# Routed attention with an MLP behind it: five small moves in an order written by hand

## The chip, the cores and the metric

The kernel runs on one core of a Trainium2 chip. The metric is the device time of one execution in microseconds (us), the median of the runs. The engines are TensorE (PE in the profile, its weight loads PEld), VectorE (DVE), ScalarE (ACT), GpSimd (POOL) and SyncE (SP); the last two mostly issue DMA transfers here.

## The reference

Attention in which every query and key is assigned to one of 16 centroids, and a query sees only the keys of its own cluster; then a layer norm and an MLP with a residual. Everything is float32.

```python
q_assign = argmax(einsum('bhsd,hcd->bhsc', q_n, c_n))     # k likewise
mask = q_assign[:, :, :, None] == k_assign[:, :, None, :]
scores = where(mask, scale * q @ k.T, -1e9)
attn = exp(scores - max); attn = attn / (sum(attn) + 1e-9)
x = (attn @ v) as (B, S, H*D)
xn = (x - mean) / sqrt(var + 1e-6) * g_ln
out = x + max(xn @ w_ch1, 0) @ w_ch2
```

B = 4 batches, H = 8 heads, S = 768 positions, D = 64 (so H*D = 512), hidden width 2048. The two MLP weights arrive as 64-bit floats.

## The kernel before, in words

**Attention.** The work is cut into 16 pairs of heads, n = 0 to 15; pair n belongs to batch n // 4. A pair has two halves ("slots" 0 and 1) of six steps. A step of a half makes one score tile of 128 keys by 384 queries for both heads: `scores` puts two mask products and two q k products into one of three PSUM buffers (`s_ps`), and ScalarE takes the exponential into `e`. `weigh` then multiplies the six tiles with v (`a_ps`), adds them up on VectorE (`es`, L433 and L436) and copies the result (`x`, L445). A half takes TensorE about ten us.

**Preparing the next pair.** While pair n is computed, pair n + 1 is prepared. Its q and k have to be turned so that D lies on the partitions. `prep_transpose` does this in one of two ways. Pairs named in `blocks` are loaded in 32 by 32 blocks, so that one VectorE transpose is enough (L281). The others are turned by six TensorE products with the identity into a score buffer (L286), which ScalarE copies (L291). k takes the first way in all pairs but pair 0. q takes it in pair 1 and in pairs 7 to 15; q of pairs 2 to 6 goes through TensorE, one pair earlier, in slot 1. `prep_sims` (`sim_ps`, L313) needs both; `prep_turn`, `prep_route`, `prep_onehot` (`oh_ps`, L355) and `prep_mask` make the one-hot and mask rows from it (`shade`, L373: on VectorE in pair 0, on ScalarE in the others).

**Closing a pair.** `finish` has four parts: 0 sums `es` over the keys on TensorE (`den_ps`) and sends the sums through DRAM into another layout; 1 takes the reciprocal and brings it back as rows (`rb`); 2 multiplies (`L488`) and stores x^T to DRAM (`xT_d`); 3 transposes and stores x (`x_d`). Parts 2 and 3 of pair n run two pairs later.

**Weights.** 32 chunks are converted from 64-bit to 32-bit floats by six VectorE operations each (`split_weight`, `join_weight`, L246 to L266) and an accumulating DMA. Two chunks go to each of pairs 0 to 6, one to each of pairs 7 to 15 (23 in all), the last nine into the first MLP layer of batch 0 (`within`).

**Norm of batch 0.** It is placed in the attention of later pairs by `put(n, slot, job)`: x^T is loaded as `xn` at pair 6, the statistics (`norm_rows`) follow at pairs 7 to 9, `norm_stats` (mean, square root on ScalarE, reciprocal) at the end of pair 9, `norm_stat_rows` between scores and weighing of pair 10, `norm_apply` at pairs 11 to 14, and the first sums of the MLP at pair 15.

**MLP.** Each layer is written with seven block products instead of eight. In `first_layer` a hidden tile j has seven parts (L761) that accumulate in banks `x_ps`, `y_ps`, `z_ps`; they need sums of x blocks (`x_sum`, L578: t1, t2, t4) and of weight blocks (`w1_sums`, L594: s1 to s4, for tile j made during tile j - 1). `first_units(0, j)` mixes in the conversions. The second layer (L854) follows, with the sums of its weights (`w2t`, L838). The norm of the next batch is hidden behind it.

**Order.** In the attention and in batch 0's first layer the order on TensorE, VectorE and ScalarE is the order of the calls (`manual_schedule`); each engine runs its queue in order. Later only TensorE's order is fixed by hand and a scheduler places the rest. The end of the attention and the start of the MLP read:

```python
finish(len(pairs) - 1, 0)
first_layer(0, 0, 1)
first_layer(0, 0, 2)
first_layer(0, 0, 6)
w1_sums(0, 0, (2, 3))
```

Of the kernel before, what the change touches and what calls it, by code (L numbers as in the profile page):

```python
# [8 lines left out]
F32 = mybir.dt.float32  # L9
# [3 lines left out]
AF = mybir.ActivationFunctionType  # L13
ALU = mybir.AluOpType
# [5 lines left out]
def kernel(  # L20
# [11 lines left out]
    nc = tc.nc  # L32
    B, H, S, D = q.shape
    NCL = centroids.shape[1]
    DM, FF = moe_w_ch1.shape
    P = 128
    NT = S // P
# [5 lines left out]
    NDC = DM // P  # L43
# [7 lines left out]
    xpool = ctx.enter_context(tc.tile_pool(name="xpool", bufs=1))  # L51
    small = ctx.enter_context(tc.tile_pool(name="small", bufs=2))
# [17 lines left out]
    def ps(name, dt=F32, n=512):  # L70
        return pools["t"].tile([P, n], dt, tag="t", name=name)

    pairs = [(b, pr) for b in range(B) for pr in range(NPAIR)]
    loaded = {n: {} for n in range(len(pairs))}

    TWICE = 7

    blocks = {
        (n, name) for n in range(1, len(pairs)) for name in ("qk" if n == 1 or n >= TWICE else "k")
    }  # L80

    def load_blocks(n, name):
# [57 lines left out]
    eps = const.tile([P, 1], F32, name="eps")  # L140
# [231 lines left out]

    def shade(n, out, src, rows):  # L373
        add, factor = far[rows, 0:1], far[rows, 1:2]
        if n:
            nc.scalar.activation(out, src, AF.Identity, bias=add, scale=factor)
        else:
            nc.vector.tensor_scalar(out, src, factor, add, op0=ALU.mult, op1=ALU.add)  # L378
# [10 lines left out]
    late = {}  # L389
# [59 lines left out]
    def finish(n, part):  # L449
        b, pr = pairs[n]  # L450
        if part == 0:
            den = ps_a.tile([P, 512], F32, tag="a", name="den_ps") if n + 1 < len(pairs) else ps("den_ps")
            for j in range(2):
                for g in range(NHALF):
                    r = (j * NHALF + g) * Q
                    nc.tensor.matmul(  # L456
                        den[r : r + Q, :HC], ones, sums[n, g][:, j, :],
                        start=True, stop=True, tile_position=(0, r),
                    )
            if n + 1 < len(pairs):  # L460
                dsb = last.tile([P, HC], F32, tag="dsb", name="dsb", bufs=1)
            else:
                dsb = late["all"][:, 1, :HC]
            nc.scalar.copy(dsb, den[:, :HC])
            flat = dram.tile([P // Q, HC], F32, tag="flat", name="flat")
            nc.gpsimd.dma_start(out=flat, in_=dsb[0:P:Q, :])
            nc.gpsimd.dma_start(
                out=rdens[:, n, :], in_=flat.rearrange("i (p e) -> (i p) e", e=DE)
            )
        elif part == 1:  # L470
            nc.vector.reciprocal(rdens[:, n, :], rdens[:, n, :])
            row = dram.tile([2, S], F32, tag="row", name="row")
            nc.gpsimd.dma_start(
                out=row.rearrange("j (p e) -> (j p) e", e=DE), in_=rdens[:, n, :]
            )
            if n + 1 < len(pairs):
                rb = last.tile([P, S], F32, tag="rb", name="rb", bufs=1)
            else:
                rb = late["all"][:, 2]
            for j in range(2):  # L480
                nc.gpsimd.dma_start(
                    out=rb[j * D : (j + 1) * D, :],
                    in_=row[j : j + 1, :].to_broadcast([D, S]),
                )
            late[n] = rb
        elif part == 2:
            a, x = xs.pop(n), late[n]
            nc.vector.tensor_tensor(x, a, x, ALU.mult)  # L488
            nc.sync.dma_start(out=xT_d[b][pr], in_=x)
        else:  # L490
            x = late.pop(n)

            if n + 1 < len(pairs):
                y = last.tile([P, S], F32, tag="y", name="y")
            else:
                y = late["all"][:, 0]
            nc.vector.transpose(y, x)
            for i in range(P // Q):
                m = pr * P + i * Q
                nc.sync.dma_start(  # L500
                    out=x_d[b].rearrange("t (a r) m -> r (t a) m", r=Q)[:, :, m : m + Q],
                    in_=y[i * Q : (i + 1) * Q].rearrange("r (g f) -> r g f", f=Q),
                )
# [3 lines left out]
    normed = {}  # L507
    rows = {}

    def norm_load(b):  # L510
        xn = xpool.tile([P, NDC, S], F32, tag="xn", name="xn")
        for c in range(NDC):
            nc.sync.dma_start(out=xn[:, c, :], in_=xT_d[b][c])
        mv = small.tile([P, NT, 2], F32, tag="mv", name="mv")
        normed[b] = [xn, mv]

    def rows_load(b, t):
        if t < NT:
# [9 lines left out]
        nc.vector.bn_stats(out=bn, in_=x)  # L528
        nc.vector.bn_aggr(out=mv[:, t, :], in_=bn)

    def norm_stats(b):

        _, mv = normed[b]
        stat = small.tile([P, 2, NT], F32, tag="stat", name="stat")
        nc.scalar.activation(stat[:, 1, :], mv[:, :, 1], AF.Sqrt, bias=eps)
        nc.vector.tensor_copy(stat[:, 0, :], mv[:, :, 0])
        nc.vector.reciprocal(stat[:, 1, :], stat[:, 1, :])
        normed[b][1] = stat

    def norm_stat_rows(b):  # L540
        sp = ps("stat_ps") if b else ps_s.tile([P, 2, 512], F32, tag="s", name="stat_ps")[:, 0]
# [55 lines left out]
    extra = {}  # L597

    def put(n, slot, f, *args):
        extra.setdefault((n, slot), []).append(lambda: f(*args))  # L600

    put(6, 0, norm_load, 0)
    put(6, 1, rows_load, 0, 0)
    put(6, 1, rows_load, 0, 1)
    for t in range(NT):
        put(7 + t // 2, t % 2, norm_rows, 0, t)
    put(9, 1, norm_stats, 0)
    put(10, "between", norm_stat_rows, 0)
    for i in range(2):
        for c in range(NDC):  # L610
            put(11 + 2 * i + c // 2, 1, norm_apply, 0, i, c)
# [10 lines left out]
    slots = per // GROUP  # L622

    convert = {}
    for n in range(len(pairs)):
        for slot in (0, 1) if n < TWICE else (0,):
            convert[n, slot] = len(convert)
    order = {mybir.EngineType.PE, mybir.EngineType.DVE, mybir.EngineType.Activation}
# [36 lines left out]
    with tc.manual_schedule(engines=order | {mybir.EngineType.Pool}):  # L665
        for u in range(len(pairs) * slots):
            n, slot = divmod(u, slots)
            nxt = n + 1 < len(pairs)
            own = range(GROUP * u, GROUP * (u + 1))
            if slot == 0 and not nxt:  # L670
                finish(n - 1, 0)
            if slot == 0 and nxt:
                for side in (1, 0):
                    if (n + 1, "qk"[side]) in blocks:
                        prep_transpose(n + 1, side)
                        load(n + 2, "qk"[side])
            for i in own:
                if i >= AHEAD:
                    scores(i)
            if slot == 0:  # L680
                if n and nxt:
                    finish(n - 1, 0)
                if nxt:
                    prep_sims(n + 1)
            elif nxt:
                prep_onehot(n + 1)
                prep_mask(n + 1, 0)
                prep_mask(n + 1, 1)
                if n + 2 < len(pairs) and (n + 2, "q") not in blocks:
                    prep_transpose(n + 2, 0)  # L690
                    load(n + 3, "q")
            for job in extra.pop((n, "between"), ()) if slot else ():
                job()
            for i in own:
                weigh(i)
            if slot and nxt:
                if n:
                    finish(n - 1, 1)
                if n > 1:
                    finish(n - 2, 2)  # L700
                    finish(n - 2, 3)
            if (n, slot) in convert:
                m = convert[n, slot]
                split_weight(m)
                join_weight(m)
                load_weight(m + 1)
            if slot == 0:
                load(n + 1, "v")
                if nxt:
                    prep_turn(n + 1)  # L710
                    prep_route(n + 1)
                else:
                    for part in (2, 3):
                        finish(n - 2, part)
                    finish(n - 1, 1)
            elif not nxt:
                for part in (2, 3):
                    finish(n - 1, part)
            for job in extra.pop((n, slot), ()):
                job()  # L720
# [31 lines left out]

    within = {}
    for m in range(len(convert), NWC):
        within.setdefault((1, 2, 3, 4, 4, 5, 5, 6, 7)[m - len(convert)], []).append(m)
    MH = DM // 2
    hidden = {}

# [164 lines left out]
                w1_sums(b, j + 1)  # L923

    with tc.manual_schedule(engines=order):
        finish(len(pairs) - 1, 0)
        first_layer(0, 0, 1)
        first_layer(0, 0, 2)
        first_layer(0, 0, 6)
        w1_sums(0, 0, (2, 3))  # L930
        x_sum(0, 3)
        first_layer(0, 0, 5)
        first_layer(0, 0, 7)
        x_sum(0, 4)
        w1_sums(0, 1)
        for j in range(1, NFH):
            first_units(0, j)
            if j in (1, 3):
                for part in ((1,), (2, 3))[j // 2]:
                    finish(len(pairs) - 1, part)  # L940
# [252 lines left out]
```

## Time and profile before

| | |
|---|---|
| time, median of 3 runs | 939.66 us (939.57 to 941.25) |
| span of the profiled execution | 936.4 us |
| busy: TensorE, VectorE, ScalarE, GpSimd | 920.6, 618.4, 348.6, 78.4 us |
| attention, up to the last `a_ps` product | 0 to 346.0 us |
| MLP of batches 0, 1, 2, 3, from | 349.8, 496.0, 640.9, 785.8 us |

The attention is full on three engines: in windows of 20 us VectorE is busy for 18 to 19 us, ScalarE for 14, and the DMA engines for 0.5 to 1.0 of the time. In the MLP TensorE has the span almost alone. Starts in the timeline are read from the beginning of the span; a group's idle time is the time its engine stood still just before it, and behind the arrow is what ended it.

### The profile page before, as it was taken

What the parts mean: (1) busy time and instruction counts of PE and PEld (TensorE: products, weight loads), DVE (VectorE), ACT (ScalarE), POOL (GpSimd) and SP (SyncE); (2) the same over time, 40 slices, a digit from 0 to 9 for tenths busy, and PEclk for the clock granted to TensorE, in tenths of its full rate; (3) what the DMA queues carried; (4) which work ended last, traced back from release to release, by engine and by line L of the source; (5) the groups of instructions that cost most, each with busy time, mean ns of one, the idle gap of its engine ahead of it and who ended that gap; (6) DMA issues with size and microseconds to landing.
All of it is one profiled execution on the core that took longest, in us unless ns stands there. A gap on an engine that the chain in (4) does not pass through costs nothing.

```text
span 936.4 us, 12611 instructions
## 1 busy us (share of the span) xinstructions
PE 920.6 (98%) x4664; PEld 589.3 (63%) x4664; DVE 618.4 (66%) x1106; ACT 348.6 (37%) x549; POOL 78.4 (8%) x146
## 2 busy tenths in 40 slices
PE   8999999998999999999999999999999999999997
PEld 5445444444444445558886557886557887556886
DVE  5989999998889987899772445372446372435331
ACT  4777767667677643331002331002332001332000
POOL 2111212211111121110000000000000000000000
PEclk9999999999999999999999999999999999999999
DMA  7577999998688445645530002120002021000011
GB/s 159 123 167 167 215 186 212 207 196 160 150 174 169 119 100 140 156 93 186 169 96 12 0 1 90 50 72 26 1 0 81 22 96 40 1 1 6 29 46 36
DMA packets 179780, 92.48 MB, mean 99 GB/s; under 512 B 145792, under 2 KB 162288, under 8 KB 179712
## 3 DMA queue, kind: packets, MB, share of 16 engines
q1 hardware_dynamic: 170368, 76.20, 33.4%
q0 software_dynamic: 7744, 15.02, 8.1%
q8 instruction: 38, 0.62, 0.3%
q10 hardware_dynamic: 1600, 0.39, 0.2%
q14 instruction: 30, 0.25, 0.1%
HBM read 64.10 MB, written 19.10 MB: 89 GB/s over the span
## 4 chain that ended last, share of the span: by engine, by line
PE 88%; DVE 8%; DMA 1%; issue 1%; SPq 1%; ACT 1%; DVEq 0%; ACTq 0%
PE x_ps L854 18%; PE x_ps L761 17%; PE s_ps L407 14%; PE a_ps L419 11%; PE z_ps L854 9%; PE z_ps L761 8%; PE y_ps L854 4%; PE y_ps L761 4%; DVE es L436 2%; PE den_ps L456 1%; PE sim_ps L313 1%; PE simT_ps L329 1%; PE oh_ps L355 1%; DVE w L261 1%; DMA v_sb<-in_v_dram 1%
## 5 line engine op out<-in xcount | busy, mean ns | idle before, releaser
L402 ACT ACTIVATE e<-s_ps 128x768 f32<-128x768 f32 x192 | 151.7, 812 | 29.3 <-PE s_ps L407 27.3
L407 PE MATMUL s_ps<-t,t 64*128 64x384 f32 x768 | 156.4, 486 | 0.0
L436 DVE TENSOR_TENSOR es<-es,e 128x768 f32<-128x768 f32 x128 | 122.7, 958 | 13.7 <-DVE es L436 0.5
L419 PE MATMUL a_ps<-e,v_sb 128*64 128x384 f32 x768 | 130.9, 490 | 0.0
L781 DVE TENSOR_TENSOR h<-z_ps,u 128x384 f32<-128x384 f32 x64 | 35.6, 556 | 92.9 <-PE z_ps L761 71.1
L419 PEld LDWEIGHTS a_ps<-e,v_sb 128*64 128x64 f32 x768 | 52.3, 137 | 69.9 <-issue 58.8
L407 PEld LDWEIGHTS s_ps<-t,t 64*128 64x128 f32 x768 | 68.7, 189 | 35.6 <-issue 35.0
L854 PE MATMUL x_ps<-w2t,h 128*128 128x256 f32 x384 | 84.5, 379 | 0.0
L789 ACT ACTIVATE h<-h 128x384 f32<-128x384 f32 x96 | 49.7, 522 | 85.4 <-DVE h L781 85.4
L854 PEld LDWEIGHTS x_ps<-w2t,h 128*128 128x128 f32 x384 | 72.7, 190 | 10.1
L407 PE MATMUL s_ps<-m,mask 64*128 64x384 bf16 x192 | 62.4, 326 | 3.3 <-ACT e L402 3.3
L407 PE MATMUL s_ps<-mask,m 64*128 64x384 bf16 x192 | 62.3, 326 | 0.4 <-DVE mask L378 0.4
L776 ACT COPY u<-x_ps 128x384 f32<-128x384 f32 x64 | 30.7, 479 | 78.0 <-PE x_ps L761 78.0
L865 DVE TENSOR_TENSOR o_sb<-x_ps,xb 128x256 f32<-128x256 f32 x48 | 20.2, 420 | 51.9 <-PE x_ps L854 51.9
L776 ACT COPY p<-x_ps 128x384 f32<-128x384 f32 x32 | 15.0, 468 | 99.4 <-PE x_ps L761 99.4
L761 PE MATMUL x_ps<-xt,ws 128*128 128x384 f32 x128 | 46.6, 487 | 0.8 <-DVE ws L594 0.8
L761 PE MATMUL x_ps<-xn,w 128*128 128x384 f32 x128 | 46.6, 487 | 0.0
L761 PE MATMUL z_ps<-xn,ws 128*128 128x384 f32 x128 | 46.5, 486 | 0.0
L761 PE MATMUL z_ps<-xt,ws 128*128 128x384 f32 x128 | 46.5, 486 | 0.0
L761 PE MATMUL x_ps<-xn,ws 128*128 128x384 f32 x128 | 46.5, 486 | 0.0
L761 PE MATMUL x_ps<-xt,w 128*128 128x384 f32 x128 | 46.5, 486 | 0.0
L761 PE MATMUL y_ps<-xn,w 128*128 128x384 f32 x128 | 46.5, 486 | 0.0
(146 smaller groups left out, 1351.4 us busy)
## 6 DMA issues: line engine op xcount, KB each, us to landing
raw<-in_moe_w_ch_dram SPq DMA_DIRECT2D x32, 512.0 KB, 4.3
w<-tb POOLq DMA_DIRECT2D x32, 256.0 KB, 5.5
v_sb<-in_v_dram SPq DMA_DIRECT2D x32, 192.0 KB, 4.4
xn<-xT_d SPq DMA_DIRECT2D x16, 384.0 KB, 5.5
xr<-x_d SPq DMA_DIRECT2D x24, 256.0 KB, 2.8
xb<-x_d SPq DMA_DIRECT2D x48, 128.0 KB, 2.2
out_dram<-o_sb SPq DMA_DIRECT2D x48, 128.0 KB, 1.7
k_sb<-in_k_dram SPq DMA_DIRECT2D x62, 96.0 KB, 5.4
```

The costliest lines, as they stand in the source:

```text
L261: nc.vector.scalar_tensor_tensor(out=w, in0=tb, scalar=float(0x38100000), in1=fa, op0=ALU.is_ge, op1=ALU.mult)
L313: nc.tensor.matmul(sim[r : r + Q, :HC], cT[:, pr, :, :].rearrange("p j c -> p (j c)"), prepared[n][side][:, g * HC : (g + 1) * HC], start= ...
L402: nc.scalar.activation(e, s[:, :, :HC], AF.Exp, scale=SCALE)
L407: nc.tensor.matmul(s[:, j, :HC], of_keys[:, keys], of_queries[:, cols], start=part == first, stop=part != first, skip_group_check=True,)
L419: nc.tensor.matmul(acc[j * D : (j + 1) * D, :HC], loaded[n]["v"][:, j, c, :], e[:, j, :], start=(c == 0), stop=(c == NT - 1),)
L436: nc.vector.tensor_tensor(es, es, soft.pop(i), ALU.add)
L761: nc.tensor.matmul(bank[:, :HC], lhs[:, c, :], rhs[:, c, :], start=first and c == 0, stop=c == NDH - 1, skip_group_check=True,)
L776: nc.scalar.copy(t, bank[:, :HC])
L781: nc.vector.tensor_tensor(h, bank[:, :HC], other, ALU.add)
L789: nc.scalar.activation(h, h, AF.Relu)
L854: nc.tensor.matmul(bank[:, :MH], hidden[lhs + (c,)][:, tt * P : (tt + 1) * P], rhs[:, c, :], start=first and c == 0, stop=c == NFH - 1, sk ...
L865: nc.vector.tensor_tensor(o, bank[:, :MH], x, ALU.add)
```

## The change

Five parts, all of them in the order of the work or in where it is done.

- The square root of batch 0's norm leaves the end of pair 9. The square root alone goes into pair 10's first half, between the scores and the weighing ("between 0"); its reciprocal comes at the end of that half, `norm_stat_rows` stays in the second half ("between 1"). It is meant to use a stretch in which ScalarE has no exponentials to do.
- The x^T of batch 0 (pairs 0 to 3) is written to its place in `xn` at once, instead of going to DRAM and back.
- The sums of the last pair (`finish(15, 0)`) come after the first two products of the MLP.
- The conversion in pair 15 is moved into the first MLP layer, which now takes ten; per tile j they are 1 at tile 1, 2 at 2, 1 at 3, 2 at 4, 1 at 5, 2 at 6, 1 at 7 (before: 1, 1, 1, 2, 2, 1, 1).
- q of pair 7 (the eighth) is turned by TensorE, not by VectorE. In pair 0, the large mask `m` is shaded by ScalarE, not by VectorE.

```diff
-        (n, name) for n in range(1, len(pairs)) for name in ("qk" if n == 1 or n >= TWICE else "k")
+        (n, name) for n in range(1, len(pairs)) for name in ("qk" if n == 1 or n > TWICE else "k")
...
-        if n:
+        if n or rows == slice(0, P):
             nc.scalar.activation(out, src, AF.Identity, bias=add, scale=factor)
...
             a, x = xs.pop(n), late[n]
-            nc.vector.tensor_tensor(x, a, x, ALU.mult)
-            nc.sync.dma_start(out=xT_d[b][pr], in_=x)
+            if b:
+                nc.vector.tensor_tensor(x, a, x, ALU.mult)
+                nc.sync.dma_start(out=xT_d[b][pr], in_=x)
+            else:
+                late[n] = norm_tiles(b)[0][:, pr, :]
+                nc.vector.tensor_tensor(late[n], a, x, ALU.mult)
...
-    put(6, 0, norm_load, 0)
...
-    put(9, 1, norm_stats, 0)
-    put(10, "between", norm_stat_rows, 0)
+    put(10, "between 0", norm_stats, 0, (0,))
+    put(10, 0, norm_stats, 0, (1,))
+    put(10, "between 1", norm_stat_rows, 0)
...
-    for n in range(len(pairs)):
+    for n in range(len(pairs) - 1):
         for slot in (0, 1) if n < TWICE else (0,):
             convert[n, slot] = len(convert)
...
-            for job in extra.pop((n, "between"), ()) if slot else ():
+            for job in extra.pop((n, f"between {slot}"), ()):
                 job()
...
-        within.setdefault((1, 2, 3, 4, 4, 5, 5, 6, 7)[m - len(convert)], []).append(m)
+        within.setdefault((1, 2, 2, 3, 4, 4, 5, 6, 6, 7)[m - len(convert)], []).append(m)
...
-        finish(len(pairs) - 1, 0)
         first_layer(0, 0, 1)
         first_layer(0, 0, 2)
+        finish(len(pairs) - 1, 0)
         first_layer(0, 0, 6)
```

## The prediction

> **What bounds the kernel now.** I read the page first (busy time, the chain that ended last), then the waits of TensorE, then the timeline around each wait. Page, busy time and chain:
>
> ```profile
> PE 920.6 (98%) x4664; PEld 589.3 (63%) x4664; DVE 618.4 (66%) x1106; ACT 348.6 (37%) x549; POOL 78.4 (8%) x146
> ...
> PE 88%; DVE 8%; DMA 1%; issue 1%; SPq 1%; ACT 1%; DVEq 0%; ACTq 0%
> ```
>
> TensorE is the kernel: only its gaps can be saved. Its waits by releaser (us in total, times, longest):
>
> ```profile
> PE s_ps L407 <- ACT e L402: 3.3, 2, 2.7
> PE den_ps L456 <- DVE es L436: 1.6, 1, 1.6
> PE sim_ps L313 <- DVE t L281: 1.1, 1, 1.1
> ...
> PE x_ps L761 <- DVE ws L594: 0.8, 1, 0.8
> ```
>
> Four single gaps; no wait repeats. The longest, at the start of pair 10, seen from ScalarE (start, duration, idle before):
>
> ```profile
> 221.08 1.28 ACT L535 ACT_TABLE_LOAD   x1
> 223.30 0.30 ACT L535 ACTIVATE stat<-mv,eps 128x6 f32<-128x6 f32 x1 [0.93 <-DVE mv L529]
> 223.61 1.28 ACT L402 ACT_TABLE_LOAD   x1
> 224.91 2.21 ACT L402 ACTIVATE e<-s_ps 128x768 f32<-128x768 f32 x3
> ...
> 235.39 0.48 ACT L445 COPY x<-a_ps 128x384 f32<-128x384 f32 x1 [3.54 <-PE a_ps L419]
> 236.84 4.79 ACT L402 ACTIVATE e<-s_ps 128x768 f32<-128x768 f32 x6 [0.98 <-PE s_ps L407]
> ```
>
> The square root stands ahead of pair 10's exponentials, waits for the last mean and variance, and has a table load on either side. TensorE fills its three score buffers and stops. The last two lines show the gap that ScalarE has in the next half pair: 3.54 us before the copy, 0.98 after it. What follows on TensorE (window, us, busy, clock, DMA share, GB/s):
>
> ```profile
> 225.80:228.80 3.00, 3.00 (x12) 0.50 0.83 186
> ```
>
> Two score tiles run at half clock after the gap. The other three gaps, in timelines of VectorE and TensorE:
>
> ```profile
> 164.16 0.94 DVE L281 STREAM_TRANSPOSE t<-q_sb 128x768 f32<-128x768 f32 x1
> ...
> 344.77 4.15 DVE L436 TENSOR_TENSOR es<-es,e 128x768 f32<-128x768 f32 x4
> ...
> 395.68 1.88 DVE L838 TENSOR_TENSOR w2t<-w 128x512 f32<-128x512 f32 x3
> ```
>
> ```profile
> 165.15 0.85 PE L313 MATMUL sim_ps<-t,cT 128*32 128x384 f32 x8 [1.10 <-DVE t L281]
> ...
> 346.58 0.83 PE L456 MATMUL den_ps<-es,ones 128*32 128x384 f32 x2 [0.58 <-ACT late L445]
> 348.98 0.85 PE L456 MATMUL den_ps<-es,ones 128*32 128x384 f32 x6 [1.56 <-DVE es L436]
> 349.75 1.56 PE L761 MATMUL x_ps<-xn,w 128*128 128x384 f32 x4
> ...
> 406.29 1.53 PE L761 MATMUL x_ps<-xt,ws 128*128 128x384 f32 x4 [0.80 <-DVE ws L594]
> ```
>
> VectorE is late in each: by pair 8's transposes, by the last exponential sums, and by the weight sums of a tile whose stage also held two conversions and the first w2t sum. Batches 1 to 3 have no TensorE wait at all: their starts, 496.04, 640.91 and 785.78, are 144.87 apart twice.
>
> **What the Trainium skill says.** "TensorE: Matmul & The Clock Gate", What's actually happening: the clock is halved after an idle window of some 3.4 us and comes back after a busy one. The trace agrees on the half (0.50) and the 3 us of it, though the gap was only 2.70. "ScalarE: Activation LUTs", What ACT_TABLE_LOAD costs: 1283 ns, and a drain of about 1380 more at each switch. The load is 1.28 in the trace; of the drain it shows nothing (load ends 224.89, exponential starts 224.91). I take 1.28 and keep the drain as a bound. "VectorE: DVE Perf Modes", The three transpose paths: TensorE's transpose goes to PSUM, VectorE's to SBUF. So the path through TensorE needs a copy: 0.80 on ScalarE here, against 0.94 on VectorE. "DMA: Bandwidth & Descriptors", Issuing engines are not separate DMA queues: all transfers share 16 engines; between 143 and 185 us their busy share is 0.96 to 1.03.
>
> **The change part by part.** Sim_ps starts at 185.46 and 205.78, then 230.47: a free pair takes 20.32, that one 24.69.
>
> (a) Square root moved into pair 10's first half, after the sim_sb copy. Its data are ready: the last statistics come before the k transposes that sim_ps waits for. Load and root, 1.28 + 0.30 = 1.58, fit in the 3.54 gap behind the twelve a_ps products. Behind the x copy stands the other load: 1.28 against 0.98 idle, so the exponentials come 0.30 late. The first would end at 237.14 + 0.81 = 237.95, and the fourth score tile needs its buffer at 235.75 + 3 x 0.81 = 238.18: TensorE does not notice. The masks end 0.3 late, at 244.8, and are needed at about 245.4. The reciprocal follows pair 10's one-hot on VectorE by 0.4; stat_ps on TensorE comes some 4 us after that. Gain 24.69 - 20.32 = 4.37: the gap with its refill, 2.9, and the half clock, 1.5. With the drain priced, the exponentials would be 1.7 late and 1.3 would be lost again.
>
> (b) Pair 7's q by TensorE. VectorE loses one transpose; from 143.42 to 165.02 it never idles, so pair 8's transposes end 0.86 earlier, at 164.2. TensorE gains six transposes: a pair that has them takes 20.98 (sim_ps at 81.13, 102.11, 123.09), one without 20.32, so +0.66. Pair 7's sim_ps comes at 123.09 + 20.98 = 144.07 instead of 143.55, pair 8's at 164.39 instead of 165.15. VectorE's 164.2 is just in time; if not, 0.1 to 0.2 stays. Gain 0.7.
>
> (c) x^T of batch 0 kept: four stores and four loads of 384 KB go, 3.1 MB in the stretch where DMA is full. The product goes straight to its place, in the same 0.9 us. No TensorE gap above ends on such a transfer, so nothing directly; raw, rb and v_sb come earlier. Worth 0.
>
> (d) Conversion of pair 15 moved, and last sums behind two products. The conversion is six VectorE operations from 335.80 to 339.1, 3.3 us. Without it the last sum ends at about 345.7, not 348.9, before TensorE's last a_ps product at 346.0; the exponentials, finished by 342.9, allow that. Then 0.58 for the late copy stays (the first product takes over that bank), two products run, 2.58, then den_ps, 0.8: the third product starts at 349.95 instead of 352.4. Its inputs (t2, s2) precede the sums on VectorE. s3 and the next x sum are due at 352.5; they follow the rb product and the y transpose, whose rb now lands about 346 (reciprocal 3 us earlier, at 337.9; row 1.8 and rb 4.9 to land by the medians of the transfers; no 256 KB weight transfer before them): ready at 351.4. Gain 2.3. Moving the sums also puts p1's copy ahead of den's on ScalarE; the den chain is only needed three tiles later.
>
> (e) That conversion in the first layer, stages now 1,2,2,3,4,4,5,6,6,7. A tile takes TensorE 9.03. VectorE has h sums 1.4, weight sums 1.5, and 3.25 a conversion: 9.4 with two, and weight sums have until 3.87 into the next tile. Stage 4 also has pair 15's product and transpose (1.9): ends 2.8 into stage 5, as in the trace. Stage 5, now with one conversion and w2t (2.5), ends 2.4 into stage 6, where the old one with two ended 5.3 in; stage 6 with two ends 2.8 into stage 7. All under 3.87, so the 0.80 wait goes, 0.96 with its refill, and none takes its place. Stage 2 with two starts from a VectorE that idled 1 to 2 us per tile there.
>
> (f) Pair 0's big mask on ScalarE, beside VectorE's two small ones: the first exponential at 14.1 instead of 14.8, but pair 1's k, landed at 16.2, and its two transposes still hold sim_ps until 18.1, against 18.2. Gain 0.1.
>
> Sum: 4.37 + 0.7 + 2.3 + 0.96 + 0.1 = 8.4. 939.66 - 8.4 = 931.3.
>
> **The rivals.** *Given back in part* (0.2): VectorE, 18.9 of 20 us busy from 100 to 220, loses the slack that the 4.37 us gap gave it, the drain is real, or the rb transfer lands late and s3 with it. Against: onehot leads oh_ps by 0.8 to 1.4 for pairs 7 to 10 and grows, pairs 11 to 14 show VectorE waiting for exponentials. One or two of these cost 1.3 to 2.5: about 933.3.
>
> *VectorE becomes the bound of the first layer* (0.08): the conversion's 3.25 is not absorbed, because raw tiles (4.3 us to land, two buffers) come late in the double stages. For: VectorE waited 0.97 for the first raw. Against: that raw was issued behind pair 14's stores, which now leave earlier. Then (e) reads +3.25 instead of -0.96: 935.5.
>
> *Slower* (0.05): p1's copy names every DMA queue among its waits. If it has to wait for pair 14's stores, as the first raw did (357.18), the third product starts at 357.2, a loss of 4.8, plus 1.5 of half clock, in place of the gain of 2.3; with the drain in (a), and pair 8 still waiting so that the 0.66 is paid for nothing, that is 939.66 - 3.1 + 0.66 - 0.96 - 0.1 + 6.3 = 942.5. Against: in the trace p1 ran at 351.35, before those stores were issued.
>
> **How the numbers follow.** The main case has 0.67, the partial one 0.2, the first layer 0.08, slower 0.05. Predicted is 931.3. The range takes the main case with the runs' own scatter (before: 939.57 to 941.25) down to 929.8, and the partial one up to 934.8; the last two are left out. Faster by over 1.9 us: 0.67 + 0.2 + 0.06 of the first-layer case, the other 0.02 of which meets the partial one and comes out even: 0.93, 0.02, and slower 0.05.
>
> **What would show it.** Right: no score wait over 0.3 us near 220 and no clock below 1 after the start; pair 8's sim_ps without a wait; x_ps directly behind the last a_ps, den_ps third, with no wait for es; no wait for ws. Wrong: a wait of s_ps for e in pair 10, of x_ps for p or xn at the start of the layer, or any ws wait in tiles 3 to 7.

## The result and the profile after

| | before | after |
|---|---|---|
| time, median | 939.97 us (938.63 to 941.25, 6 runs) | 932.25 us (930.67 to 933.90, 6 runs) |
| span of the profiled execution | 936.4 us | 929.1 us |
| TensorE busy, share of the span | 920.6 us, 98% | 918.7 us, 99% |
| traffic of the DMA queues | 92.48 MB | 89.35 MB |

The ratio is 0.9917, with a 95% interval of 0.9901 to 0.9934: the changed kernel is 0.8% faster. The forecast was 931.3 us, 8.4 below; the medians are 7.7 apart, the two traces 7.3. Two more series of six runs gave 931.61 and 931.98.

The page of the changed kernel, its busy line and the chain that ended last:

```profile
PE 918.7 (99%) x4670; PEld 589.1 (63%) x4670; DVE 614.6 (66%) x1104; ACT 349.8 (38%) x551; POOL 78.3 (8%) x146
...
PE 92%; DVE 3%; DMA 3%; issue 1%; SPq 1%; ACT 0%; DVEq 0%; ACTq 0%
```

TensorE still is the kernel. VectorE's share of the chain fell from 8% to 3%. The waits of TensorE after the change (us in total, times, longest):

```profile
PE s_ps L407 <- ACT e L402: 1.2, 2, 0.6
PE idle_ps L649 <- DVE warm L168: 1.0, 1, 1.0
PE s_ps L407 <- DVE mask L378: 0.7, 2, 0.4
PE x_ps L774 <- ACT late L445: 0.6, 1, 0.6
PE den_ps L456 <- ACT x L445: 0.6, 1, 0.6
PE sim_ps L313 <- DVE t L281: 0.6, 1, 0.6
```

The waits for `es` (1.6) and for `ws` (0.8) are gone and the longest score wait fell from 2.7 to 0.6. But the wait for `t` is still there (0.6, from 1.1), and there are still two score waits for `e`: one of them is at the start of the kernel, as before, the other is new. ScalarE's timeline shows where that one is from:

```profile
227.91 1.28 ACT L545 ACT_TABLE_LOAD   x1
229.21 0.30 ACT L545 ACTIVATE stat<-mv,eps 128x6 f32<-128x6 f32 x1
231.44 0.48 ACT L445 COPY x<-a_ps 128x384 f32<-128x384 f32 x1 [1.93 <-PE a_ps L419]
232.88 1.28 ACT L402 ACT_TABLE_LOAD   x1 [0.96 <-PE s_ps L407]
234.17 4.33 ACT L402 ACTIVATE e<-s_ps 128x768 f32<-128x768 f32 x6
```

The root lies in the gap as it should, and nobody waits for it. The table load behind it (L402) does not start when the copy ends at 231.92: it stands idle for 0.96 until a score product is done, and only then loads. The exponentials come 1.28 late, where the forecast had 0.30, and the new score wait, 0.64, is TensorE's.

To see where the 7.3 us are, the span is cut at starts that belong to fixed work: `sim_ps` of pairs 0, 1, 8 and 15 (it opens the preparation of a pair), and the first xt product of batch 1's MLP. Each part is the distance between two such starts, read from the timeline of TensorE:

```
part of the span              before    after   after - before
start to sim_ps of pair 0       8.51     8.39    -0.12
sim_ps of pair 0 to pair 1      9.69    10.29    +0.60
pair 1 to pair 8              146.95   146.90    -0.05
pair 8 to pair 15             146.72   143.11    -3.61
pair 15 to batch 1            186.58   183.37    -3.21
the rest                      437.95   437.04    -0.91
```

So the two large parts carry the gain, the third (pair 7's q) gave next to nothing in this trace, and the start got longer. One trace is one execution, and the series below show how much the second part differs between executions: the trace of before is the shortest of the four with pair 7's q on VectorE and all transfers (146.95, 147.01, 149.14, 151.40). The rest, nearly all of it MLP, was 436.8 to 438.0 us in all the kernels below, with the edits and without: its 0.9 is put down to no edit here.

### The profile page after: what moved, and what is told of

It is laid out like the page before. It is cut to its first block, busy times and chain, and to the rows that moved or that the text cites. A ratio compares the mean times of both kernels' runs of the same rounds, so it can differ in the third digit from the quotient of the medians.

```text
span 929.1 us, 12604 instructions
## 1 busy us (share of the span) xinstructions
PE 918.7 (99%) x4670; PEld 589.1 (63%) x4670; DVE 614.6 (66%) x1104; ACT 349.8 (38%) x551; POOL 78.3 (8%) x146
## 2 busy tenths in 40 slices
DMA packets 177061, 89.35 MB, mean 96 GB/s; under 512 B 144096, under 2 KB 160592, under 8 KB 176992
## 4 chain that ended last, share of the span: by engine, by line
PE 92%; DVE 3%; DMA 3%; issue 1%; SPq 1%; ACT 0%; DVEq 0%; ACTq 0%
PE x_ps L867 18%; PE x_ps L774 18%; PE s_ps L407 13%; PE a_ps L419 12%; PE z_ps L867 9%; PE z_ps L774 9%; PE y_ps L867 4%; PE y_ps L774 4%; PE den_ps L456 1%; DMA v_sb<-in_v_dram 1%; PE sim_ps L313 1%; DVE es L436 1%; DMA raw<-in_moe_w_ch_dram 1%; PE simT_ps L329 1%; PE oh_ps L355 1%
## 5 line engine op out<-in xcount | busy, mean ns | idle before, releaser
L402 ACT ACTIVATE e<-s_ps 128x768 f32<-128x768 f32 x192 | 151.6, 811 | 24.3 <-PE s_ps L407 21.8
```

The source lines that it names most:

```text
L402: nc.scalar.activation(e, s[:, :, :HC], AF.Exp, scale=SCALE)
```

## The experiments

Two questions came out of the traces. Which edit earns what, since three of them touch the same stretch? And why did pair 7's q bring nothing? The table at the end of this section has the same parts for all runs.

**The square root alone**, on the kernel before:

```diff
...
-    put(9, 1, norm_stats, 0)
-    put(10, "between", norm_stat_rows, 0)
+    put(10, "between 0", norm_stats, 0, (0,))
+    put(10, 0, norm_stats, 0, (1,))
+    put(10, "between 1", norm_stat_rows, 0)
...
```

> The kernel before with the square root's move alone. Theory A (the second table load carries the wait of the exponential behind it, so it does not start before that exponential's score tile is ready, 1.28 late): the interval between the pairs that holds the root falls from 24.69 to about 20.3, the next one rises from 20.42 to about 21.2, TensorE keeps one score wait of about 0.6 behind that table load, and the third product of the first layer starts 3.5 to 3.7 us earlier than before. Rival B (the late start comes from the other parts: work or transfers that the kept x^T or pair 7's q displaced): the second load starts right behind the copy, the next interval stays 20.4, and the full 4.37 us is gained.

Measured: at the place of the edit all as Theory A had it. The intervals between the pairs are 20.31 and 21.23 (before: 24.69, 20.42), and pairs 8 to 15 take 143.16. Yet the kernel as a whole took 941.27 us beside 940.84 for the kernel before, and the third product of the first layer came 3.35 later than before, not 3.5 earlier. The gain was eaten elsewhere, at two places that the edit does not touch. One is on VectorE, in the pairs with two conversions:

```profile
131.75 0.43 DVE L246 TENSOR_SCALAR ta<-raw 128x512 uint32<-128x512 uint32 x1 [4.09 <-DMA raw<-in_moe_w_ch_dram]
```

A raw chunk (`raw` holds a chunk of the 64-bit weights as it arrives) was late by 4.09 us; pairs 1 to 8 took 151.40, 4.45 more than in the trace of before. The other is at the head of the MLP. TensorE waits there for 0.58 and 1.56 us, exactly as before, but what follows differs. Stretches of TensorE behind the wait, of this kernel (window, us, busy, clock, DMA share, GB/s):

```profile
352.00:354.00 2.00, 2.00 (x4) 0.50 0.04 15
```

and of the kernel before:

```profile
350.00:352.00 2.00, 2.00 (x7) 1.00 0.01 2
```

The same wait let the clock fall to half in one execution and not in the other; the later batch 1 start (188.24 against 186.58) is that, 1.66 us.

**The early table load**, on the changed kernel: one exponential of a 128x1 tile right behind the root.

```diff
             nc.scalar.activation(stat[:, 1, :], mv[:, :, 1], AF.Sqrt, bias=eps)
+            if b == 0:
+                nc.scalar.activation(warm, warm, AF.Exp, scale=0.0)
```

> The changed kernel with one small exponential (a 16-element-or-so tile, its result unused) right behind the square root, so that the second table load has no score tile to wait for. Theory A (the load waited with the exponential): that load lies in the 3.54 us gap behind the root, the exponentials of pair 10's second half start within 0.1 us of their score tile, the 0.64 us score wait goes, the interval of 21.23 becomes 20.3 to 20.5, and everything after is about 0.8 us earlier. Rival B (the half pair is late because of the clock, the masks or the transposes): the load moves but the interval stays at 21.0 or more, with another wait in place of the score wait.

Measured, ScalarE's timeline of this kernel:

```profile
230.03 0.30 ACT L545 ACTIVATE stat<-mv,eps 128x6 f32<-128x6 f32 x1
230.35 1.28 ACT L547 ACT_TABLE_LOAD   x1
231.64 0.20 ACT L547 ACTIVATE warm<-warm 128x1 f32<-128x1 f32 x1
232.26 0.48 ACT L445 COPY x<-a_ps 128x384 f32<-128x384 f32 x1 [0.42 <-PE a_ps L419]
233.72 4.79 ACT L402 ACTIVATE e<-s_ps 128x768 f32<-128x768 f32 x6 [0.97 <-PE s_ps L407]
```

The load now runs ahead of the copy, both fit in the gap with 0.42 to spare, and the exponentials wait for scores and not for a table. The new score wait is gone and the interval is 20.42 instead of 21.23. This is Theory A for the exponential: its load waited for its scores. It is no rule for every table load: in the prediction's lines the square root's own load ran at 221.08, at once, and only the root itself waited for `mv` (0.93). Batch 1's root in the kernel before shows it at length:

```profile
428.74 1.28 ACT L535 ACT_TABLE_LOAD   x1
447.39 0.30 ACT L535 ACTIVATE stat<-mv,eps 128x6 f32<-128x6 f32 x1 [17.37 <-DVE mv L529]
```

Why the one load waits and the other does not was not tried. (In this run late raw chunks cost 1.07 us more before pair 8 than in the first trace of the changed kernel, so that the span is 929.1 all the same.)

**The last sums alone, and the conversion alone**, each on the kernel before:

```diff
-        finish(len(pairs) - 1, 0)
         first_layer(0, 0, 1)
         first_layer(0, 0, 2)
+        finish(len(pairs) - 1, 0)
```

> The kernel before with only the last pair's sums moved behind the first two products; the conversion stays in pair 15. Theory A (the sums and the conversion have to move together): the wait of den_ps for es (1.56) goes, but the sums on VectorE end as late as before, so the reciprocal and its transfer are late too, and a wait of the same kind comes at the first product that needs rb or s3: the first layer's later tiles start less than 1 us earlier than before. Rival B (the order on TensorE alone is enough): 2.2 to 2.5 us are gained by the second tile of the first layer.

```diff
-    for n in range(len(pairs)):
+    for n in range(len(pairs) - 1):
...
-        within.setdefault((1, 2, 3, 4, 4, 5, 5, 6, 7)[m - len(convert)], []).append(m)
+        within.setdefault((1, 2, 2, 3, 4, 4, 5, 6, 6, 7)[m - len(convert)], []).append(m)
```

> The kernel before with only pair 15's conversion moved into the first layer; the last sums stay ahead of the products. Theory A (VectorE's 3.3 us in pair 15 made the wait, the order on TensorE adds little): the 1.56 us wait for es goes with the conversion, the ws wait of 0.80 goes as well, and the sums' order is worth 0.7 us at most: about 2.3 + 0.96 us gained at the end of the first layer. Rival B (the order is needed: es still comes late at the head, since exponentials and not the conversion end it): a wait of den_ps for es of 0.5 us or more stays, and the gain by the second tile is under 1.5 us.

Measured with the sums moved alone, TensorE at the head of the MLP:

```profile
350.48 0.85 PE L456 MATMUL den_ps<-es,ones 128*32 128x384 f32 x8
351.26 1.56 PE L761 MATMUL x_ps<-xt,ws 128*128 128x384 f32 x4
...
356.06 2.35 PE L761 MATMUL x_ps<-xn,ws 128*128 128x384 f32 x4 [1.95 <-DVE xn L578]
```

and VectorE:

```profile
351.97 0.96 DVE L488 TENSOR_TENSOR rb<-x,rb 128x768 f32<-128x768 f32 x1 [1.93 <-DMA rb<-row]
352.96 0.98 DVE L497 STREAM_TRANSPOSE y<-rb 128x768 f32<-128x768 f32 x1
...
354.96 0.95 DVE L578 TENSOR_TENSOR xn<-xn 128x768 f32<-128x768 f32 x1
```

The wait for `es` is gone and the third product starts 2.3 earlier within its stretch. Two products later the gain is lost: VectorE, 3.3 us late through the conversion, asked for the reciprocal rows late, waits 1.93 for them, and everything in its queue behind that (transpose, s3, the x sum) waits too. TensorE stands for 1.95: its fifth product starts 143.1 after `sim_ps` of pair 15, as in the kernel before. That is Theory A: nothing gained. It comes back at half clock (four products take 2.35 instead of 1.45), and batch 1 starts after 188.29, 1.7 later than in the trace of before. That loss can't be put down to the order: with the root alone, where the order is the old one, the waits at this place also ended in half clock and batch 1 in 188.24.

Measured with the conversion moved alone, TensorE:

```profile
347.43 0.85 PE L456 MATMUL den_ps<-es,ones 128*32 128x384 f32 x8 [0.58 <-ACT late L445]
348.22 1.56 PE L761 MATMUL x_ps<-xn,w 128*128 128x384 f32 x4
```

No wait for `es`, none for `ws`, none of VectorE for the reciprocal rows, batch 1 after 183.17: a gain of 3.41, more than the 3.21 of both edits together. So the conversion carries (d) and (e), and the order of sums and products costs 0.2 where it was thought to help.

**Pair 7's q without the transfers.** In the changed kernel VectorE's queue showed two waits for raw ahead of pair 8, 1.27 and 0.29 us. Two kernels take the transfers of conversions 1 to 13 away and keep all VectorE work; they convert the first chunk again, so those weights are left out:

```diff
+        kept = raws[0]
...
-                load_weight(m + 1)
+                if m < 13:
+                    raws[m + 1] = kept
+                else:
+                    load_weight(m + 1)
```

The second of them also has `n >= TWICE` again, so that q of pair 7 is turned by VectorE.

> The changed kernel without the raw loads of conversions 1 to 13: they work again on the first chunk, so those weights are left out, and every VectorE operation stays. Theory A (raw's landing took pair 7's gain): no raw wait, pair 8's transposes end before TensorE is ready, the sim_ps wait of 0.55 goes, and the stretch from pair 6's to pair 8's sim_ps is 41.3 (20.98 + 20.32) as forecast. Rival B (VectorE is short of time there anyway): a sim_ps wait of 0.3 or more stays and the stretch is 41.8 or more.

> As the kernel with one raw chunk, with pair 7's q transposed by VectorE as before. It shows what pair 7's q is worth when no transfer interferes. Theory A: pair 8's sim_ps waits for t by about 1.1 and the stretch from pair 6 to pair 8 is about 42.0, 0.7 longer than with q on TensorE. Rival B: VectorE has slack enough without late chunks, the wait goes here too, and the stretch is 40.7 to 41.0, shorter than with q on TensorE because six transposes (0.66) are missing there.

Measured with q on TensorE, and then with q on VectorE:

```profile
164.46 0.83 PE L313 MATMUL sim_ps<-t,cT 128*32 128x384 f32 x8
```

```profile
165.41 0.85 PE L313 MATMUL sim_ps<-t,cT 128*32 128x384 f32 x8 [1.08 <-DVE t L281]
```

The stretch from pair 6 to pair 8 is 41.29 in the first (123.17 to 164.46) and 41.90 in the second (123.51 to 165.41). Both are Theory A: without late chunks q on TensorE is worth 0.6, six products more against a wait of 1.08 less.

**The changed kernel again, twice.** No edit; the runs show what differs between executions of one program.

> The changed kernel once more, unaltered, for a second trace. Theory A (in the pairs with two conversions VectorE depends on when each 512 KB raw chunk lands in its single buffer, and that differs between runs of the same program): the starts from pair 3 to pair 8 differ by up to 1 us or more from the first trace, with other raw waits, while everything fixed by instruction order stays: 21.23 for the half pair behind the second table load, 2.3 from the moved sums and conversion, tiles of 9.03. Rival B (the changed program itself delays raw in a fixed way): the same raw waits of 1.27 and 0.29 at the same conversions, the same 165.58 within 0.2.

> The changed kernel a third time, as the comparison for the two below and for a third trace of its starts. Theory A (raw chunks land earlier or later from run to run): again another set of raw waits, and the start of pair 8's sim_ps less that of pair 1's somewhere from 146.2 to 149, never below 146.2; 21.23 behind the second table load as ever. Rival B: 146.9 as in the first trace.

Measured: pairs 1 to 8 took 147.99 and 148.16 (first trace 146.90), with raw waits of 0.71 and 1.30 in the one and 2.19 and 0.65 in the other. Pairs 8 to 15 and the way to batch 1 repeat to 0.02. From the second trace:

```profile
149.81 0.43 DVE L246 TENSOR_SCALAR ta<-raw 128x512 uint32<-128x512 uint32 x1 [1.30 <-DMA raw<-in_moe_w_ch_dram]
```

```profile
166.45 0.85 PE L313 MATMUL sim_ps<-t,cT 128*32 128x384 f32 x8 [1.64 <-DVE t L281]
```

The sizes differ as Theory A has it, and pair 8 starts 0.9 and 1.1 later than in the first trace. But not all of it is chance, and here Rival B has a part: the second wait of each trace (0.29, 1.30, 0.65) is at the same conversion, the first of pair 6. Of the eight traces with q of pair 7 on TensorE and all transfers six have a wait there (0.20 to 2.63), of the four with it on VectorE none. VectorE, rid of that transpose of 0.94, comes to this conversion earlier, which would explain it; this was not tried apart. There is one raw buffer in this stretch, so the next chunk is asked for only when the last one is converted, and VectorE has hardly any idle time in which to take the delay up.

**x^T through DRAM again**, on the changed kernel: the product is stored, and the four loads at pair 6 are back.

```diff
...
-                late[n] = norm_tiles(b)[0][:, pr, :]
-                nc.vector.tensor_tensor(late[n], a, x, ALU.mult)
+            nc.vector.tensor_tensor(x, a, x, ALU.mult)
+            nc.sync.dma_start(out=xT_d[b][pr], in_=x)
...
+    put(6, 0, norm_load, 0)
```

> The changed kernel with batch 0's x^T stored to DRAM and loaded again as before. Theory A (the kept x^T is worth nothing on TensorE's path): from pair 8's sim_ps to pair 15's 143.1 as in the changed kernel, no wait for xn, only scatter before pair 8. Rival B (3.1 MB less traffic is what brings raw and rb in time): raw waits of over 1.5 us in pairs 4 to 7 or a wait for xn or rb later, 1 us or more lost.

Measured: 143.12 from pair 8 to 15, 183.36 to batch 1, no wait for `xn`: nothing on that path, as Theory A says. Before pair 8 one raw chunk was 2.63 late and the stretch 148.99 long. That is Rival B's number. The kernels before and with one edit alone have the same x^T transfers; they have no raw wait at this conversion, but up to 4.09 at others. So one run does not decide whether less traffic makes raw more punctual.

**Putting it together.** The early table load as above, and pair 0's large mask back on VectorE (the early load's lines are left out here):

```diff
-        if n or rows == slice(0, P):
+        if n:
```

> The changed kernel with the small exponential behind the square root and pair 0's large mask back on VectorE. If the table load's wait (0.81) and the two readers of one PSUM tile (about 0.3 at the first exponential) are what they seem, it is 0.8 to 1.1 us faster than the changed kernel, some 931.2 beside 932.2, with no score wait near pair 10; if the mask's place is not what delays the start, 0.8.

Measured: 930.16 us beside 931.61 for the changed kernel and 938.93 for the one before in the same series (0.9911, 0.9893 to 0.9929). The runs of this kernel (928.90 to 932.76) and of the changed one (929.75 to 933.89) overlap, so what the two edits earn is read from the traces: 0.80 for the load, up to 0.39 for the mask. VectorE in pair 0, of the changed kernel first, then of this one:

```profile
11.03 0.56 DVE L340 SCALAR_TENSOR_TENSOR onehot<-simT_ps,best 128x384 bf16<-128x384 f32 x1
...
13.29 1.38 DVE L378 TENSOR_SCALAR mask<-oh_ps,far 16x768 bf16<-16x768 bf16 x2 [1.69 <-ACT m L376]
```

```profile
10.88 0.56 DVE L340 SCALAR_TENSOR_TENSOR onehot<-simT_ps,best 128x384 bf16<-128x384 f32 x1
...
12.05 0.68 DVE L378 TENSOR_SCALAR m<-oh_ps,far 128x768 bf16<-128x768 bf16 x1 [0.61 <-PE oh_ps L355]
12.75 1.38 DVE L378 TENSOR_SCALAR mask<-oh_ps,far 16x768 bf16<-16x768 bf16 x2
```

With `m` on ScalarE (0.99 there) VectorE's masks do not run beside it but wait for its end: from the one-hot to the last mask 3.64 instead of 3.25. Where pair 1's k lands early enough, this is what the way from pair 0 to pair 1 is made of: never below 10.08 us with `m` on ScalarE, 9.69 with `m` on VectorE. Where k lands late, it hides the difference (its transpose starts between 15.8 and 17.1 in these runs; in the first trace of the changed kernel it starts at 16.79, late enough to set the 10.29 by itself).

Then the sums ahead of the products again, and in the last kernel pair 6's second conversion moved into the first layer too (the sums' lines are left out here):

```diff
-        for slot in (0, 1) if n < TWICE else (0,):
+        for slot in (0, 1) if n < TWICE - 1 else (0,):
...
-        within.setdefault((1, 2, 2, 3, 4, 4, 5, 6, 6, 7)[m - len(convert)], []).append(m)
+        within.setdefault((1, 1, 2, 2, 3, 4, 4, 5, 6, 6, 7)[m - len(convert)], []).append(m)
```

> The kernel with the early table load and pair 0's mask on VectorE, and the last sums ahead of the two products again. Theory A (the moved conversion alone removes the es wait; the products before the sums buy nothing): no es wait, and the first layer starts its second batch 183.2 us after pair 15's sim_ps, 0.2 earlier than the 183.4 of the changed kernel. Rival B (the order of sums and products is what removes the wait): an es wait of 0.5 us or more, second batch at 184.0 or later. In all some 1.0 to 1.3 us faster than the changed kernel.

> The same, and pair 6's second conversion moved into the first layer as well (eleven there, two in each of the first two stages). Theory A (VectorE has no slack in the pairs with two conversions, so a late raw chunk costs TensorE time there): pair 8's sim_ps waits for no t even where a raw chunk is late, the stretch from pair 1 to pair 8 stays at 146.2 to 146.6, and the time is 0.5 to 1 us below that of the kernel with ten. Rival B (the first layer can't take an eleventh conversion): a ws or xn wait in tiles 1 to 6 that gives 1 us or more back.

Measured: 930.40 us with ten conversions in the layer and 929.31 with eleven, beside 931.98 for the changed kernel and 939.45 for the one before (ratios 0.9910, 0.9893 to 0.9927; and 0.9891, 0.9875 to 0.9907). The first of them overlaps with the changed kernel's runs. The sums' old place is worth its 0.2 (183.17 to batch 1), and no `es` wait comes back. With eleven, raw chunks were late by 0.78 and 0.31 and no `sim_ps` after pair 1's waited: pair 8's had 2.7 us in hand. The last kernel's slowest run, 929.62, is below the changed kernel's fastest in that series, 929.95, and its runs lie within 1.3 us, the other's within 5. Its chain of waits:

```profile
PE 98%; SPq 1%; DMA 0%; DVE 0%; ACT 0%; issue 0%
```

The parts of the span in all of these runs, in us:

```
kernel                      pair 0-1   1-8     8-15    15-batch 1
before                        9.69   146.95   146.72   186.58
root alone                   10.34   151.40   143.16   188.24
sums alone                   10.39   149.14   145.24   188.29
conversion alone             10.73   147.01   146.91   183.17
after                        10.29   146.90   143.11   183.37
after, second trace          10.13   147.99   143.13   183.36
after, third trace           10.43   148.16   143.11   183.37
early table load             10.08   147.97   142.31   183.36
x^T through DRAM             10.08   148.99   143.12   183.36
one raw, q on TensorE        10.08   146.17   143.13   183.36
one raw, q on VectorE        10.08   146.78   143.19   183.36
early load, mask back         9.69   146.16   142.31   183.36
and sums first                9.82   147.16   142.31   183.17
and eleven in the layer      10.18   146.17   142.30   183.18
```

## Why the prediction was right, and where its steps were off

The forecast held: TensorE's single gaps were the thing to read, and the two largest terms of the sum came from the edits that were named for them. That the total came so near is in part luck: of the 7.3 us between the two traces 0.9 lies in the rest, where no edit acts, and what lies before it is 6.4, against a forecast of 8.4. By its steps:

- **(a), the square root: mechanism right, size off by 0.8.** The gap, its refill and the half clock went (24.69 to 20.31, as forecast), and the masks and the reciprocal held nobody up. The term that failed is "the exponentials come 0.30 late ... TensorE does not notice". It let the table load start behind the copy; it started with its exponential's score, 1.28 late, and the next interval grew from 20.42 to 21.23. The gain is 3.6, not 4.37, and 1.5 of it, the half clock, was not lost in every execution of a kernel with the old gap (last section). "ScalarE: Activation LUTs", What ACT_TABLE_LOAD costs, has a drain of about 1.38 on top of the load; the trace shows none (the load ends at 234.16, the exponential starts at 234.17; with the early load, the root ends at 230.33 and the load starts at 230.35). So the rival that priced a loss of 1.3 by the drain was right that something is lost here, from a cause that is not in the trace. A sign that was to show the forecast wrong, a score wait for `e` in pair 10, did come, with 0.64.
- **(b), pair 7's q: right as a trade, forecast 0.7, worth 0.6 and mostly not seen.** The term was sized from a trace in which raw was late by only 0.22 in that stretch. In the first trace after, the chunks took it (0.05 gained from pair 1 to 8); in the kernel with the early load and the mask back, with all transfers, raw was late by only 0.35 and the stretch took 146.16, 0.8 less than before. The text had named the raw chunks as a danger for the first layer, not for this pair. The sign that was to show it right, pair 8's `sim_ps` without a wait, appeared only where raw was on time.
- **(c), x^T kept: worth 0 from pair 8 on, as said.** Whether the traffic matters for raw stays open.
- **(d) and (e): size right (3.26 forecast, 3.21 measured), but one half of (d) was credited wrongly.** The conversion's 3.3 us on VectorE were the whole cause; the sums behind the products are not needed and cost 0.2. With the sums first batch 1 starts after 183.17 or 183.18, with them behind after 183.36 or 183.37; the traces put the 0.2 in the first products, of which only one takes 1.39 to the next start with the sums first (the others 1.29), and three take 1.39 with the sums between them. So the two products of the forecast, 2.58, took 2.78. Why was not tried. The forecast's own starts, 349.95 instead of 352.4, give 2.45, and it entered 2.3; measured were 2.29.
- **(f), the mask: sign wrong.** The step took "beside VectorE's two small ones" for granted, and they run one behind the other, up to 0.39 later. Both engines read the tile `oh_ps`. "PSUM — Partial Sum Buffer", Terms, says that two engines may not be in one bank and quadrant at once, "reads against reads included". That fits the wait in the trace; no run gave the two engines a bank each, so it is argued and not shown.
- **The rivals.** "Given back in part" came true in small: (a) lost 0.8, raw lost what (b) won. VectorE did not become the bound of the first layer, not even with eleven conversions; p1's copy never waited for stores.

## What to carry to other kernels

Where an engine has no slack, an edit's value is what is left after the transfers' scatter: look for the step that asks for its next transfer only when the last is used up, and give that stretch slack, before counting tenths. When two edits hide one wait, try each alone; here one did all the work and the other, alone, only moved the wait. A table switch can come late although its engine is idle: a small operation of the new table, with nothing to wait for, right behind the last one of the old brought it forward here. And a stretch that scatters by microseconds is compared over several traces, not over one of each kernel.

## What the runs showed of the hardware that was not expected

- A table load can wait for the inputs of the instruction behind it, but need not. The load ahead of an exponential stood idle for 0.96 us until that exponential's scores were there (232.88), and the same load ahead of an exponential with no inputs to wait for ran at once (230.35). The load ahead of batch 1's square root ran at once (428.74), and the root behind it then waited 17.37 us for its input.
- TensorE's clock after one and the same gap differs between executions. The score wait of 2.70 us was followed by 3 us at half clock in the kernel before, and again with the conversion moved alone (that interval took 24.88); with the sums moved alone, which leaves that gap as it was, the wait was 2.71 and the clock stayed at 1.00 (pairs 8 to 15 took 145.24 there, not 146.72). The waits of 0.58 and 1.56 at the head of the MLP did it the other way about, full clock before and half with the root alone. A wait of 1.95 also halved it. "TensorE: Matmul & The Clock Gate", What's actually happening, has an idle window of some 3.4 us that runs free of the kernel. That the outcome changes from run to run agrees with it; the length does not, since every one of these idle times is below it.
- The 512 KB chunks of raw weights were up to 4.1 us late for VectorE in one execution (the root alone) and 0.2 us in another (before) of kernels that load them alike in that stretch.
